# A chunked linear-attention and cosine-FFN kernel: first loads in thirds, no running minimum, the last output in halves, and another written order for the first stage

## The chip, the cores and the metric

The kernel runs on one core of one Trainium2 chip. The metric is the device time of one execution in microseconds (us), and lower is better. The core has five engines that run their own instruction streams and wait for each other through semaphores: TensorE (PE, matrix products), VectorE (DVE), ScalarE (ACT), GpSimd (POOL), and SyncE (SP), which here only issues DMA transfers. DMA transfers go through queues that feed 16 DMA engines. Matrix products write to PSUM, and everything else works from SBUF.

## The reference: what is computed

The first half is a recurrent attention over 768 steps for 4 batches and 8 heads with head size 48. Each step decays a 48x48 state and adds an outer product. The second half is a feed-forward layer with `h * cos(h)` between two matrix products, over 3072 tokens. All of it is fp32.

```python
for t in range(S):                                   # S = 768
    kt, vt, rt, wt = (k[:, :, t], v[:, :, t], r[:, :, t], w[:, :, t])
    cur = np.einsum('bhd,bhe->bhde', u[None] * kt, vt)
    y[:, :, t] = np.einsum('bhd,bhde->bhe', rt, state + cur)
    state = wt[:, :, :, None] * state + np.einsum('bhd,bhe->bhde', kt, vt)
...
x = y.transpose(0, 2, 1, 3).reshape(B * S, H * D)    # 3072 x 384
h = x @ w_in                                         # 384 -> 2048
return (h * np.cos(h)) @ w_out                       # 2048 -> 384
```

## The kernel before

**Tiling.** The 768 steps of a batch are cut into 6 chunks of 128 steps, so there are 24 chunks (numbered 0 to 23 in the order of work, with the batches of a pair alternating). Two chunks make a block of 256 tokens, and there are 12 blocks. Inside a chunk the recurrence becomes matrix products: cumulative products of the decays scale `r` and `k`, a 128x128 score matrix per head covers the chunk itself, and a 48x48 state per head carries what came before.

**Attention steps of a chunk,** by the short names that the order tables use:

- `load`: one DMA of 112 rows by 1541 floats (L185). A row holds `r` (512 floats), `k` (512) and the decays (517), in this order.
- `decay` (L203 to L220): `rkt` = r times k (L205, chunks 0 to 5 alone), a scan from the right for the decays to the chunk's end (`ee`, L208), the smallest product so far (`shrink`, L211), the whole product with a floor (`whole`, L213), its reciprocal (`inj`, L214), a second scan (L215), r times the second scan (L219), and k times the first (L220). L208 to L215 run on DVE. In the first stage L219 is on DVE and L220 on POOL.
- `diag`: products with `u` (PE, L226), a copy to `cd` (ACT), and two POOL instructions (L238) that lay them on a diagonal in `asb`.
- `a`: 8 products for the scores (PE, L258, written to `pa`), then two DVE instructions (L260) that put the masked scores into `asb`.
- `t`, `d`, `s`: the transpose of k (PE, L267, `pt`), the decayed state (`dd`), and the new state (PE, L285, `pst`).
- `o`, `p`, `x` of a block: own and past outputs (PE, L315 and L325, `py`), copied to `yf`, sent by DMA to the layout of the feed-forward layer (`xf`, L334 and L301), and split into a high and a low part (`xT`).

**Feed-forward units.** The 2048 hidden columns are 16 weight tiles of 128, and two tiles make a unit. `mm1` of a unit is 18 products (L382) into a PSUM tile `ph`. The gate of this unit follows: ACT rounds (L357), DVE subtracts (L358), ACT takes a sine and a square (L359, L360), and DVE multiplies (L361). Then ACT (or DVE later) takes the high part `gs`, and POOL the low part (L137, L140). `mm2` is 12 products (L398) into an accumulator. There are 96 units. They are numbered here from 0 in the order of mm1, and "gate 11" is L357 to L361 of unit 11.

**Weights.** A weight tile comes by DMA as doubles (`f` in the tables, tile `raw`, L147) and is converted once (`w`, L149 to L174). Two ACT instructions read the raw words (L159, L161), three DVE instructions build an fp32 (L163, L164, L171), ACT takes its high part and DVE its low part (L140). Raw tiles lie in slots that later hold converted weights. The raw tile of the last weight tile takes the slot of the raw tile before it, so its load waits until L164 and L161 have read that one.

**Stages and what sets the order.** In the first stage all 16 weight tiles are converted while blocks 0 and 1 take turns (`PAIR`), each unit running as soon as its weights are there. `START` is a table of step names, written by hand, that sets in which order the steps are recorded. PE and SP keep this order exactly. The instructions of DVE, ACT and POOL are placed by a scheduler from the same recording. After `START`, the table `PLAN` repeats for each block, and PE alone keeps its order.

While the two blocks take turns, `ph` has two PSUM banks, so mm1 of unit n writes where unit n-2 was, and waits for L361 of gate n-2. `mm1` runs ahead of `mm2` by a few units.

**The end.** After the last mm2 the two accumulators of the block are scaled and copied out (L405 to L412): chunk 0 of the block by ACT, the last chunk by DVE, each followed by one DMA from SP. A check near the end (`take_vote`, L486 to L496) tells by one number whether any decay product fell under a floor or any decay was above 1. If so, a slow path (`one_by_one`) recomputes everything. With these inputs it doesn't run.

## Time and profile before

| | |
|---|---|
| median of 3 runs | 572.2 us (572.1 to 574.48) |
| profiled execution, its own time | 578.14 us |
| span of the profiled execution | 576.3 us |
| mean granted TensorE clock | 0.961 |
| busy: PE, DVE, ACT, POOL | 525.4, 417.3, 248.5, 243.1 us |
| instructions | 11206 |
| DMA | 56.07 MB, mean 97 GB/s |

A profile shows one execution. "Busy" is the time in which an engine executed something. The granted clock is the share of its full speed that TensorE's clock was given, and matrix products take longer where it is low. A row of a timeline gives the start, the time from the first start to the last end, the engine, the line, the operation, what it writes and reads, and a count. In brackets stands the idle time just ahead of it with what ended it. A DVE instruction may start some 0.1 us before the one in front of it has ended, so the cost of a short one is read from the distance between starts.

### The profile page before, as it was taken

To read this page: it belongs to the slowest core of one execution; us is meant where nothing else is said; L and a number is where in the kernel's file an instruction comes from. 1 tells how busy PE (TensorE), PEld (TensorE's weight loads), DVE (VectorE), ACT (ScalarE), POOL (GpSimd) and SP (SyncE) were. 2 spreads that over 40 slices of the span, in tenths; PEclk is the share of its full clock that TensorE was granted. 3 is DMA by queue.
4 is the path that set the end of the run, shared out by engine and by line. 5 is a ranking of instruction groups with operands and counts; after the bars stand their busy time and mean duration, and the time that the engine had idled before them with its cause. 6 is when DMAs were issued, how large, how long until landed. Compare 5 with 4: busy or idle time off the path is not lost.

```text
span 576.3 us, 11206 instructions
## 1 busy us (share of the span) xinstructions
PE 525.4 (91%) x4420; PEld 501.7 (87%) x4420; DVE 417.3 (72%) x695; ACT 248.5 (43%) x419; POOL 243.1 (42%) x288
## 2 busy tenths in 40 slices
PE   3627888979999999899999999999899999999997
PEld 2516788979899999899899999899799999999996
DVE  6999999993786956955858847846857848836342
ACT  2355777852534342342442342342343342435441
POOL 2224238473534534532734633543444542313332
PEclk9966898986999999999999999999999999999999
DMA  8738384100434205215233025025015016310000
GB/s 262 237 107 318 96 305 116 54 3 28 145 118 134 74 28 155 52 39 158 59 110 105 2 75 160 1 61 172 3 53 155 1 43 229 115 42 16 27 1 31
DMA packets 22983, 56.07 MB, mean 97 GB/s; under 512 B 4240, under 2 KB 15120, under 8 KB 22928
## 3 DMA queue, kind: packets, MB, share of 16 engines
q1 hardware_dynamic: 20336, 53.55, 29.8%
q10 hardware_dynamic: 2592, 1.77, 1.2%
q8 instruction: 36, 0.59, 0.4%
q14 instruction: 19, 0.16, 0.1%
HBM read 45.87 MB, written 4.72 MB: 88 GB/s over the span
## 4 chain that ended last, share of the span: by engine, by line
PE 65%; DVE 16%; DMA 9%; issue 3%; SPq 2%; ACT 2%; POOL 1%; ACTq 0%; DVEq 0%; POOLq 0%
PE acc L398 26%; PE ph L382 26%; DMA xf<-yf 5%; PE py L315 5%; PE pa L258 4%; DMA tt<-tr 4%; DVE ee L208 2%; DVE tt L215 2%; PE py L325 2%; SPq L301 2%; DVE h L164 2%; DVE w L140 1%; DVE h L171 1%; DVE rr L361 1%; PE pt L267 1%
## 5 line engine op out<-in xcount | busy, mean ns | idle before, releaser
L140 POOL TENSOR_TENSOR gs<-rr,gs 128x256 fp32r<-128x256 f32 x192 | 165.3, 882 | 215.1 <-DVE gs L137 165.7
L382 PE MATMUL ph<-xT,w 128*128 128x256 f32 x1728 | 228.3, 288 | 18.0 <-ACT xT L137 10.0
L382 PEld LDWEIGHTS ph<-xT,w 128*128 128x128 f32 x1728 | 219.3, 194 | 21.9 <-ACT xT L137 10.1
L398 PE MATMUL acc<-w,gs 128*128 128x384 f32 x1152 | 222.9, 342 | 9.1 <-DVE gs L137 4.9
L398 PEld LDWEIGHTS acc<-w,gs 128*128 128x128 f32 x1152 | 200.3, 192 | 14.5 <-DVE gs L137 5.9
L359 ACT ACTIVATE rr<-rr 128x512 f32<-128x512 f32 x96 | 60.7, 632 | 120.5 <-DVE rr L358 120.5
L357 ACT ACTIVATE rr<-ph 128x512 int32<-128x512 f32 x96 | 56.5, 589 | 122.4 <-PE ph L382 82.1
L361 DVE SCALAR_TENSOR_TENSOR rr<-rr,ph 128x512 f32<-128x512 f32 x96 | 65.5, 682 | 49.7 <-ACT rr L360 49.0
L358 DVE SCALAR_TENSOR_TENSOR rr<-rr,ph 128x512 f32<-128x512 int32 x96 | 65.3, 680 | 33.9 <-ACT rr L357 33.7
L360 ACT ACTIVATE rr<-rr 128x512 f32<-128x512 f32 x96 | 60.6, 631 | 2.4
L238 POOL TENSOR_SCALAR_AFFINE_SELECT asb<-cd 128x512 f32<-128x512 f32 x48 | 35.0, 754 | 30.0 <-PE py L315 16.2
L137 DVE CAST gs<-rr 128x512 fp32r<-128x512 f32 x80 | 37.5, 469 | 9.9 <-PE acc L398 9.6
L208 DVE TENSOR_TENSOR_SCAN ee<-tt,one_e 112x516 f32<-112x516 f32 x24 | 30.4, 1267 | 15.6 <-DMA tt<-tr 15.2
L258 PE MATMUL pa<-tt 48*128 48x128 f32 x384 | 33.4, 311 | 3.5 <-DVE tt L219 3.5
L258 PEld LDWEIGHTS pa<-tt 48*128 48x128 f32 x384 | 28.2, 210 | 9.2 <-issue 3.0
L219 POOL TENSOR_TENSOR tt<-tt 112x512 f32<-112x512 f32 x18 | 24.1, 1337 | 27.8 <-DVE tt L215 27.8
L260 DVE COPY_PREDICATED asb<-mask,pa 128x512 f32<-128x512 uint8 x48 | 33.4, 731 | 0.9 <-PE pa L258 0.9
L215 DVE TENSOR_TENSOR_SCAN tt<-tt,inj 112x516 f32<-112x516 f32 x24 | 33.6, 1401 | 0.1
L315 PE MATMUL py<-asb,v 128*64 128x128 f32 (+1 forms) x384 | 27.3, 300 | 1.3 <-DVE asb L260 1.3
L315 PEld LDWEIGHTS py<-asb,v 128*64 128x64 f32 (+1 forms) x384 | 23.5, 143 | 3.9 <-DVE asb L260 2.6
L220 POOL TENSOR_TENSOR tt<-tt,ee 112x512 f32<-112x512 f32 x6 | 9.6, 1599 | 35.6 <-DVE ee L208 29.0
L231 DVE TENSOR_TENSOR rk<-rk 128x384 f32<-128x384 f32 x18 | 10.0, 559 | 15.9 <-DMA rk<-tn 15.9
(67 smaller groups left out, 353.5 us busy)
## 6 DMA issues: line engine op xcount, KB each, us to landing
tt<-tr SPq DMA_DIRECT2D x24, 674.2 KB, 6.1
raw<-wts SPq DMA_DIRECT2D x16, 768.0 KB, 8.2
rk<-tn SPq DMA_DIRECT2D x18, 384.0 KB, 3.9
v<-tn SPq DMA_DIRECT2D x24, 192.0 KB, 5.0
out<-ob SPq DMA_DIRECT2D x24, 192.0 KB, 2.0
ww<-w SPq DMA_DIRECT2D x6, 768.0 KB, 4.3
xf<-yf SPq DMA_DIRECT2D x30, 72.0 KB, 2.2
xf<-yf ACTq DMA_DIRECT2D x18, 72.0 KB, 4.2
```

The source lines that it names most:

```text
L140: E[name].tensor_tensor(out=out, in0=full, in1=high.bitcast(F32), op=ALU.subtract)
L208: nc.vector.tensor_tensor_scan(out=ee.rearrange("p a t -> p (a t)")[:, ::-1], data0=wp[:, 1:W129 + 1][:, ::-1], data1=one_e.rearrange("p a ...
L215: nc.vector.tensor_tensor_scan(out=wp[:, 0:W129], data0=wp[:, 0:W129], data1=inj.rearrange("p a t -> p (a t)"), initial=0.0, op0=ALU.mult, ...
L258: nc.tensor.matmul(out=pa[h][:, p], lhsT=a["k3"][rows(h), p], rhs=a["r3"][rows(h), p], start=True, stop=True)
L315: nc.tensor.matmul(out=py[SWAPPED[p]][ROW * o:ROW * o + m, n, p // 2], lhsT=a["v"][:, head_cols(p, h, m)], rhs=a["asb", h][:, p], start=n ...
L357: nc.scalar.activation(nn, ph, AF.Copy, scale=INV2PI / W_SCALE)
L358: nc.vector.scalar_tensor_tensor(out=rr, in0=nn, scalar=-2.0 * math.pi * W_SCALE, in1=ph, op0=ALU.mult, op1=ALU.add)
L359: nc.scalar.activation(rr, rr, AF.Sin, scale=0.5 / W_SCALE)
L360: nc.scalar.activation(rr, rr, AF.Square)
L361: nc.vector.scalar_tensor_tensor(out=rr, in0=rr, scalar=-0.5, in1=ph, op0=ALU.add, op1=ALU.mult)
L382: nc.tensor.matmul(out=ph[:, fi], lhsT=wgt[u * FU + fi][:, 0, a, kt * 128:(kt + 1) * 128], rhs=xT[:, b, kt], start=n == 0, stop=n == 3 * K ...
L398: nc.tensor.matmul(out=accs[i][j][:, :DM], lhsT=gs[:, a, fi, j * C:(j + 1) * C], rhs=wgt[u * FU + fi][:, 1, b], start=u == 0 and fi == 0 a ...
```

## The change

1. `shrink`, its start value and its instruction of each chunk (L211) are gone. Each chunk's whole product (L213) goes to its own columns of a tile `wholes` that stays, and the check at the end takes the smallest of them all in one instruction and compares it with the floor.
2. The loads of chunks 0 and 1 are three transfers each: the decays first, then `k`, then `r`. All other loads stay one transfer.
3. The last chunk's output is scaled in two halves at the same time, 192 columns by DVE and 192 by ACT, and each half has a DMA of its own, one issued by SP and one by ACT.
4. The table `START` has another order. Transposes `t2` and `t4`, scores `a4`, states `d0` and `d3`, some weight steps, one load and the outputs `o2` stand at other places.

```diff
+IN_PARTS = 2
...
-START = ["lv0 decay0 diag0 t0 load0 f load1 d0 f a0 f f diag1 w t1 decay2 o0 w a1 f diag2 d1 x0 f load3 p0 f",
+START = ["lv0 decay0 diag0 t0 load0 f load1 f d0 a0 f f diag1 w t1 decay2 o0 w a1 f diag2 d1 x0 f load3 p0 f",
...
-         "w lv4 w mm1 load6 mm1 lr6 t4 mm2 a4 w d4 mm2 w mm1 w mm1 w mm1 diag5 a5 w mm2 lv6 f mm2 mm1 d5 x4 o2",
+         "w lv4 w mm1 lr6 t4 mm2 a4 mm1 w d4 w load6 mm2 w mm1 w mm1 mm1 diag5 a5 mm2 lv6 w f mm2 mm1 d5 x4",
...
-    shrink = cst.tile([R, NP], F32, name="shrink")
-    nc.vector.memset(shrink, 1.0)
+    wholes = cst.tile([R, NG, NP], F32, name="wholes")
...
-        E["qt"].dma_start(out=tt, in_=tr[g])
+        for cols in ((1024, TRW), (512, 1024), (0, 512)) if j < IN_PARTS else ((0, TRW),):
+            E["qt"].dma_start(out=tt[:, slice(*cols)], in_=tr[g, :, slice(*cols)])
...
-        nc.vector.tensor_tensor(out=shrink, in0=shrink, in1=ee[:, :, 0], op=ALU.min)
-        whole = buf("whole", [R, NP], F32)
+        whole = wholes[:, a["j"]]
         nc.vector.tensor_single_scalar(out=whole, in_=ee[:, :, 0], scalar=LEAST, op=ALU.max)
...
-                        nc.vector.tensor_scalar(out=ob, in0=accs[i][j][:, :DM], scalar1=-2.0 / W_SCALE ** 2, scalar2=None, op0=ALU.mult)
+                        nc.vector.tensor_scalar(out=ob[:, :DM // 2], in0=accs[i][j][:, :DM // 2], scalar1=-2.0 / W_SCALE ** 2, scalar2=None, op0=ALU.mult)
+                        nc.scalar.activation(ob[:, DM // 2:], accs[i][j][:, DM // 2:DM], AF.Copy, scale=-2.0 / W_SCALE ** 2)
...
+                if at_end and j:
+                    nc.sync.dma_start(out=out[chunk * C:(chunk + 1) * C, :DM // 2], in_=ob[:, :DM // 2])
+                    nc.scalar.dma_start(out=out[chunk * C:(chunk + 1) * C, DM // 2:], in_=ob[:, DM // 2:])
+                else:
+                    E["qo"].dma_start(out=out[chunk * C:(chunk + 1) * C, :], in_=ob)
...
-        low = cst.tile([R, NP], F32, name="low")
-        nc.vector.tensor_single_scalar(out=low, in_=shrink, scalar=LEAST, op=ALU.is_lt)
+        least = cst.tile([R, 1], F32, name="least")
+        nc.vector.tensor_reduce(out=least, in_=wholes.rearrange("p g a -> p (g a)"), axis=mybir.AxisListType.X, op=ALU.min)
+        low = cst.tile([R, 1], F32, name="low")
+        nc.vector.tensor_single_scalar(out=low, in_=least, scalar=LEAST, op=ALU.is_le)
```

What moves is shown at three places. In the changed kernel the lines of the decay step carry other numbers: L206 is the old L205, and L209 the old L208.

**The first instructions of DVE,** after its constants are set. Before:

```order
L205 TENSOR_TENSOR rkt<-tt 112x512
L208 SCALAR_TENSOR_TENSOR ee<-tt,one_e 112x516
L211 TENSOR_TENSOR shrink<-shrink,ee 112x4
L213 TENSOR_SCALAR whole<-ee 112x4
L214 RECIPROCAL inj<-whole 112x4
L215 SCALAR_TENSOR_TENSOR tt<-tt,inj 112x516
L219 TENSOR_TENSOR tt<-tt 112x512
L109 TENSOR_REDUCE halves<-ident 96x2
L102 CAST mask<-maskf 128x512
L163 TENSOR_SCALAR h<-h 128x768
```

Now:

```order
L209 SCALAR_TENSOR_TENSOR ee<-tt,one_e 112x516
L213 TENSOR_SCALAR wholes<-ee 112x4
L214 RECIPROCAL inj<-wholes 112x4
L215 SCALAR_TENSOR_TENSOR tt<-tt,inj 112x516
L206 TENSOR_TENSOR rkt<-tt 112x512
L219 TENSOR_TENSOR tt<-tt 112x512
L110 TENSOR_REDUCE halves<-ident 96x2
L103 CAST mask<-maskf 128x512
L209 SCALAR_TENSOR_TENSOR ee<-tt,one_e 112x516
L163 TENSOR_SCALAR h<-h 128x768
```

Both scans of chunk 0 stand ahead of `rkt`, and chunk 1's first scan stands ahead of the first weight tile's L163 where it stood behind two of its instructions.

**PE between the scores of chunks 2 and 3.** `pc` and `pa` are chunk 3's diagonal products and the scores of chunk 2, then of chunk 3. `pt` is the transpose of chunk 2. Before:

```order
L226 MATMUL pc<-u_by_head,rkt 128x2 x4
L258 MATMUL pa<-tt 128x128 x8
L267 MATMUL pt<-ident,tt 128x112 x4
L258 MATMUL pa<-tt 128x128 x8
L315 MATMUL py<-asb,v 64x128
```

Now:

```order
L267 MATMUL pt<-ident,tt 128x112 x4
L382 MATMUL ph<-xT,w_176 128x256 x9
L382 MATMUL ph<-xT,w_236 128x256 x9
L226 MATMUL pc<-u_by_head,rkt 128x2 x4
L258 MATMUL pa<-tt 128x128 x16
L315 MATMUL py<-asb,v 64x128
```

The transpose went ahead of the first mm1, and the two sets of scores now follow each other.

**DVE between gate 10 and gate 11,** from behind L361 of gate 10 to L361 of gate 11. `w_1160` before and `w_1110` now are the low part of the last weight tile. Before:

```order
L260 COPY_PREDICATED asb<-mask,pa 128x512 x2
L163 TENSOR_SCALAR h<-h 128x768
L208 SCALAR_TENSOR_TENSOR ee<-tt,one_e 112x516
L164 SCALAR_TENSOR_TENSOR h<-raw,sign_bit,h 128x768
L211 TENSOR_TENSOR shrink<-shrink,ee 112x4
L213 TENSOR_SCALAR whole<-ee 112x4
L171 ISA h<-h,rd 128x1536
L214 RECIPROCAL inj<-whole 112x4
L358 SCALAR_TENSOR_TENSOR rr<-rr,ph 128x512
L215 SCALAR_TENSOR_TENSOR tt<-tt,inj 112x516
L140 TENSOR_TENSOR w_1160<-h,w_1160 128x2x384
L361 SCALAR_TENSOR_TENSOR rr<-rr,ph 128x512
```

Now:

```order
L171 ISA h<-h,rd 128x1536
L358 SCALAR_TENSOR_TENSOR rr<-rr,ph 128x512
L214 RECIPROCAL inj<-wholes 112x4
L209 SCALAR_TENSOR_TENSOR ee<-tt,one_e 112x516
L140 TENSOR_TENSOR w_1110<-h,w_1110 128x2x384
L215 SCALAR_TENSOR_TENSOR tt<-tt,inj 112x516
L361 SCALAR_TENSOR_TENSOR rr<-rr,ph 128x512
```

The two score copies (L260), L163, L164, a whole product and `shrink` no longer stand between the two gates. The copies, L163 and L164 now stand between gates 9 and 10. Chunk 7's whole product, reciprocal and second scan come behind gate 11; the reciprocal and the second scan that stand here now are chunk 6's.

Behind the first stage the written orders are the same in both kernels, but for a few instructions of one pair of chunks on DVE, the check near the end, and the last output.

7 lines of the change are left out of this document (3 added, 4 removed), and 6 rows, old and new, of the table START.

## The prediction

> **What bounds the kernel now.** I read the slices of the page first, then the clock by stretches, then the timelines around the one place where they all meet.
>
> ```profile
> PE   3627888979999999899999999999899999999997
> DVE  6999999993786956955858847846857848836342
> PEclk9966898986999999999999999999999999999999
> ```
>
> One slice is 14.4 us. DVE is full for nine slices, to about 130 us, and PE isn't. From the tenth slice on PE is full and DVE isn't. So the first 126 us belong to DVE and the rest to PE. Work taken from DVE pays in the first part alone, and there only where PE waits for it. The clock row has its last dip at the seam, in slice 10.
>
> ```profile
> 81.07:84.48 3.41, 2.08 (x18) 1.91 (x17) 3.41 (x9) 2.81 (x6) 0.00 (x0) 1.00 0.92 294
> 84.48:91.30 6.82, 6.82 (x52) 6.64 (x53) 6.82 (x10) 6.17 (x11) 5.68 (x4) 1.00 0.93 262
> 91.30:94.70 3.40, 1.57 (x12) 1.40 (x12) 3.40 (x5) 1.62 (x4) 3.40 (x4) 0.96 0.39 93
> 94.70:98.10 3.40, 3.40 (x18) 3.40 (x17) 3.32 (x4) 2.12 (x5) 3.40 (x3) 0.54 0.03 5
> ...
> 125.40:139.10 13.70, 12.83 (x58) 12.62 (x59) 8.62 (x16) 4.21 (x9) 4.82 (x5) 0.51 0.09 30
> ```
>
> The columns are the stretch, its length, busy time of PE, of PE's loads, DVE, ACT and POOL, then the granted clock. Where PE idled 1.33 us of 3.41, the clock stayed at 1.00. Where it idled 1.83 of 3.40, the next 3.4 us ran at about half. From 125.40 on it was at half for 13.7 us, behind the pause that is shown next. So here the point at which a pause costs clock lies between 1.33 and 1.83 us of such a stretch.
>
> ```profile
> 86.57 0.95 PE L226 MATMUL pc<-u_by_head,rkt 112*128 112x2 f32 x8
> ...
> 112.86 1.16 PE L258 MATMUL pa<-tt 48*128 48x128 f32 x16
> ...
> 120.45 2.25 PE L398 MATMUL acc<-w,gs 128*128 128x384 f32 x12
> 126.27 4.18 PE L382 MATMUL ph<-xT,w 128*128 128x256 f32 x18 [3.57 <-DVE rr L361]
> 130.25 1.70 PE L226 MATMUL pc<-u_by_head,rkt 112*128 112x2 f32 x8
> 131.88 2.40 PE L258 MATMUL pa<-tt 48*128 48x128 f32 x16
> 134.21 6.53 PE L398 MATMUL acc<-w,gs 128*128 128x384 f32 x24
> 140.58 2.31 PE L382 MATMUL ph<-xT,w 128*128 128x256 f32 x18
> ```
>
> This is the seam. mm1 of unit 13 waits 3.57 us for gate 11, then PE works without a gap but at half clock. The pause costs itself and then 4.18 - 2.31 on this mm1, 1.70 - 0.95 on `pc`, 2.40 - 1.16 on `pa` and 6.53 - 2 x 2.25 on two mm2, 5.9 us together. Nothing else is late here, so all of it is on the path. From here on PE sets the end, and whatever the start of this mm1 gains, the kernel gains.
>
> **The change part by part.** All is counted at the start of that mm1.
>
> *The removed minimum.*
>
> ```profile
> 7.79 0.17 DVE L211 TENSOR_TENSOR shrink<-shrink,ee 112x4 f32<-112x4 f32 x1
> 7.87 2.35 DVE L213 TENSOR_SCALAR whole<-ee 112x4 f32<-112x4 f32 x1
> ...
> 16.27 1.80 POOL L220 TENSOR_TENSOR tt<-tt,ee 112x512 f32<-112x512 f32 x1 [6.08 <-DVE ee L208]
> 16.95 1.14 DVE L211 TENSOR_TENSOR shrink<-shrink,ee 112x4 f32<-112x4 f32 x1
> ```
>
> ```profile
> L211 DVE TENSOR_TENSOR shrink<-shrink,ee 112x4 f32<-112x4 f32 x8 | 5.3, 667 | 0.0
> ```
>
> The last row is the group of these instructions in the first 135 us, 5.3 us over 8. This isn't what the removal saves. The instruction takes a step of 0.08 us when nothing is in its way (7.79 to 7.87). At 16.95 it took 1.14 us, until POOL's L220, begun at 16.27, was over at 18.07. At 7.87 the same delay fell on L213, 2.35 us. So the delay belongs to POOL's instruction, and the next one on DVE inherits it. I count 8 x 0.08 = 0.64 us, with 5.3 as the upper bound.
>
> *The order of DVE ahead of gate 11.* In the new order DVE does the same work ahead of L361 of gate 11, less the eight minima and less chunk 7's whole product, reciprocal and second scan.
>
> ```profile
> 116.88 0.66 DVE L361 SCALAR_TENSOR_TENSOR rr<-rr,ph 128x512 f32<-128x512 f32 x1
> 117.46 1.38 DVE L260 COPY_PREDICATED asb<-mask,pa 128x512 f32<-128x512 uint8 x2
> 118.73 0.54 DVE L163 TENSOR_SCALAR h<-h 128x768 int32<-128x768 int32 x1
> ...
> 120.33 0.99 DVE L164 SCALAR_TENSOR_TENSOR h<-raw,sign_bit,h 128x768 int32<-128x768 int32 x1
> ...
> 123.46 1.22 DVE L215 TENSOR_TENSOR_SCAN tt<-tt,inj 112x516 f32<-112x516 f32 x1
> 124.61 0.93 DVE L140 TENSOR_TENSOR w<-h,w 128x768 fp32r<-128x768 f32 x1
> 125.45 0.67 DVE L361 SCALAR_TENSOR_TENSOR rr<-rr,ph 128x512 f32<-128x512 f32 x1
> ```
>
> The scan's step is 124.61 - 123.46 = 1.15, the whole product's 0.08 and the reciprocal's about 0.1. With the minima that is **1.95 us** less. The order also evens the gates out. From gate 10 to gate 11 DVE took 125.45 - 116.88 = 8.57 us. Without the copies (118.73 - 117.46 = 1.27), L163 (about 0.5), L164 (about 0.9) and the short ones it is about 5.8. PE has an mm1 and an mm2 to do in this time, some 4.4 us warm. The pause ahead of the mm1 thus falls from 3.57 to about 1.4 us, next to the 1.33 that cost no clock.
>
> *A new wait on ACT and DVE.* Gate 10 now shares its stretch with the last weight tile, whose load can only start when L164 of the tile ahead has read the slot.
>
> ```profile
> 111.73 0.33 SPq L147 DMA_DIRECT2D raw<-wts  x1
> ```
>
> ```profile
> 117.46 0.93 ACT L159 ACTIVATE h<-raw 128x768 f32<-128x768 f32 x1 [1.88 <-DMA raw<-wts]
> ```
>
> From the issue to L159 it took 5.73 us, and L163 needs L159. In the new order only about 6.2 us of DVE work lie between that L164 and this L163: two low parts of weights (0.84 each), the two copies (1.27), a first scan (like the second, 1.15), L171 (like L164, 0.9), L361 and L358 (0.6 each). Against it stand 6.7 us for the load and L159. On ACT the sine of gate 10 also stands behind L159 and L161. DVE then waits 0 to 1.5 us. I take **0.7 lost**. Queued behind it are the L361 of gates 10 and 11, for which mm1 of units 12 and 13 wait.
>
> *The first loads.*
>
> ```profile
> tt<-tr SPq DMA_DIRECT2D x3, 674.2 KB, 11.3
> ```
>
> ```profile
> 2.68 0.43 SPq L185 DMA_DIRECT2D tt<-tr  x1
> ...
> 5.92 0.69 DVE L205 TENSOR_TENSOR rkt<-tt 112x512 f32<-112x512 f32 x1 [3.84 <-DMA tt<-tr]
> ...
> 10.96 0.89 ACT L159 ACTIVATE h<-raw 128x768 f32<-128x768 f32 x1 [2.23 <-DMA raw<-wts]
> ...
> 12.83 0.55 DVE L163 TENSOR_SCALAR h<-h 128x768 int32<-128x768 int32 x1
> ```
>
> The decays of chunk 0 land some 2 us ahead of the whole (a third of the bytes), and with that DVE starts near 4 instead of 5.92. But it doesn't keep this. Its next scan is chunk 1's. This load was issued at 2.68 and landed 11.3 later (the middle one of the three in the first 30 us), at 14.0, behind the first weight tile, which landed by 10.96. A third of these 3 us puts the decays of chunk 1 at 12.0. DVE then has the same list in front of it that it began at 12.83, so the gain is **0.8 us**. It is 0 if the third lands late, and no more than 1.9, the lead at the start.
>
> *The transpose between two scores.*
>
> ```profile
> 52.31 1.01 PE L267 MATMUL pt<-ident,tt 112*128 112x112 f32 x4 [2.91 <-DVE asb L260]
> ```
>
> ```profile
> 55.66 1.33 DVE L260 COPY_PREDICATED asb<-mask,pa 128x512 f32<-128x512 uint8 x2 [0.88 <-PE pa L258]
> ```
>
> DVE idled 0.88 us for the second scores, and a transpose of 1.01 us stood ahead of them. The second half of these scores still needs a bank that DVE's copy frees, so I take **0.7** of the 0.88.
>
> *The end.*
>
> ```profile
> 572.49 0.56 DVE L408 TENSOR_SCALAR ob<-acc 128x384 f32<-128x384 f32 x1 [3.68 <-PE acc L398]
> ```
>
> ```profile
> out<-ob SPq DMA_DIRECT2D x24, 192.0 KB, 2.0
> ...
> xf<-yf ACTq DMA_DIRECT2D x18, 72.0 KB, 4.2
> ```
>
> Half the columns save at most half of 0.56. A whole output took 2.0 us to land, and I leave it at that. From ACT's queue even 72 KB took 4.2, so up to 2.2 us may be lost. I take **0.2 gained**.
>
> *The clock.* If the pause stays under the point, the half clock goes. In this profile it cost 5.9 us. The stretches of 3.4 us don't move with the program: had one begun with the mm1, a single cold one (94.70 to 98.10) might have ended it, at 1.7. I take the middle, **3.8**.
>
> The sum is 1.95 - 0.7 + 0.8 + 0.7 + 0.2 + 3.8 = 6.75 us. The profiled execution, at 578.14, would be 571.4. It lies 5.9 us above the median of the three runs (572.2), and the share of the clock in that can't be seen, which is one more reason for the middle. Of the median the sum makes **565.4**.
>
> Which pauses count is where the Trainium skill ("TensorE: Matmul & The Clock Gate", What's actually happening) differs. It lets the clock fall after at least one idle window of about 3.4 us, in windows that run freely. The free windows agree with the rows; the length doesn't, since 1.83 us of idling was enough here. By its rule the new pause could not cost clock and the old one just could, and the sum would have 5.9 where it has 3.8: 563.3.
>
> **The rivals.**
>
> 1. *No pause counts any more, and the old one cost all of 5.9.* For it: the pause of 1.33 us. Against it: 1.4 is near 1.83, and a lost us on DVE closes the distance. Time: 572.2 - 2.95 - 5.9 = **563.3**. The clock page's rule would give this too.
> 2. *The pause shrinks but still costs clock.* Then the terms without the clock stay: 572.2 - 2.95 = **569.2**. For it: DVE's delays behind POOL are about 1.1 us each, and one of them between gates 10 and 11 makes 1.4 into 2.5.
> 3. *DVE's gain is used up.* Delays behind POOL and the wait for the last weight tile reach their bounds (another 0.8 and two delays of 1.1): 572.2 - 2.95 + 3.0, about **572**. That is also what is left if the removals do nothing beyond their 0.08 us steps and the order merely shuffles.
> 4. *Slower, by the last weight tile.* If its load takes 2 us longer than 5.7, gate 10 is late by 2, and the pause moves ahead of mm1 of unit 12, where it counts. It decides from 1.8 us on. This mm1 and the next mm2 then run cold: 4.2 instead of 2.3, and 4.4 instead of 2.25. mm1 of unit 13 starts about 2 us later than before, and the cold stretch after it is the same. With 1 us lost at the end by ACT's queue: **575.2**.
>
> **How the numbers follow.** The forecast (565.4) has 0.40, rival 1 0.13, rival 2 0.23, rival 3 0.13, rival 4 0.11. About 0.5% (2.9 us) is what a measurement of this kernel can tell from no change, so faster means under 569.3. The first two are faster, and of rival 2 a little over half: 0.40 + 0.13 + 0.13 = 0.66. Rival 4 is slower at 0.11. The rest, 0.23, is the same. The range runs from the 563.3 of rival 1 less 1.8 for a larger gain at the removed minima and first loads, 561.5, to 572.0, which takes in rival 2 and most of rival 3. The likeliest case by itself spans 563 to 568.
>
> **What would show it.** Right: the first scan starts near 4 us; the idle time ahead of unit 13's mm1 is below 2 us and the mm1 starts near 123.3; the clock there reads 1.00; PE's busy time falls by some 6 us while the counts stay. The removed minima's delays reappear on L213 or L164. Wrong: a low clock after 120 us, an L163 or an L361 of gate 10 with idle time ahead of it that a load or ACT ended, or a last DMA that lands over 2.5 us after its issue. If mm1 of unit 13 starts early and the time doesn't follow, then something behind it sets the end, and the reading of the first two rows was wrong.

## The result and the profile after

| | before | changed |
|---|---|---|
| median of 20 runs each | 573.7 us (570.05 to 577.79) | 568.8 us (562.83 to 572.63) |
| ratio | | 0.991, 95% interval 0.9888 to 0.9931 |
| profiled execution, its own time | 578.14 us | 567.22 us |
| span | 576.3 us | 565.4 us |
| mean granted TensorE clock | 0.961 | 0.970 |
| busy: PE, DVE | 525.4, 417.3 us | 522.6, 414.5 us |

The changed kernel is faster by 4.9 us, 0.9%. Here and below the ratios leave out executions that took over 1.5% longer than the fastest of the same kernel (up to four of a kernel; one, with the minimum back, took 656 us), while the medians have them all. The two profiled executions differ by 10.9 us, so more than half of what a comparison of the two traces shows isn't the change. The slices of the changed kernel's page:

```profile
PE   2637988989999999899999999999999999999997
DVE  5899899997787956856859758849858749836342
PEclk9965699999999999999999999999999999999999
```

The dip of the clock at the seam (slice 10) is gone. Another one, from 33 to 67 us, has become longer. DVE is still full to the ninth slice.

The seam on PE in the changed kernel's timeline:

```profile
118.64 2.38 PE L382 MATMUL ph<-xT,w 128*128 128x256 f32 x18
120.85 2.28 PE L398 MATMUL acc<-w,gs 128*128 128x384 f32 x12
124.82 2.37 PE L382 MATMUL ph<-xT,w 128*128 128x256 f32 x18 [1.69 <-DVE rr L361]
127.03 0.95 PE L226 MATMUL pc<-u_by_head,rkt 112*128 112x2 f32 x8
...
130.35 4.44 PE L398 MATMUL acc<-w,gs 128*128 128x384 f32 x24
134.62 2.29 PE L382 MATMUL ph<-xT,w 128*128 128x256 f32 x18
```

mm1 of unit 13 starts at 124.82 (126.27 before). Its pause is 1.69 us (3.57), and what stands behind it runs at its warm lengths: 2.37 instead of 4.18, 0.95 instead of 1.70, 4.44 instead of 6.53. Unit 14's mm1, 14.31 us behind unit 13's before, now is 9.80 behind it. The clock of the 14 us from 126 on, by stretch (length, busy PE, PE's loads, DVE, ACT, POOL, clock, DMA share, GB/s), before:

```profile
126.00:140.00 14.00, 13.73 (x63) 13.52 (x64) 8.02 (x15) 4.21 (x8) 5.01 (x7) 0.54 0.09 29
```

and changed:

```profile
126.00:140.00 14.00, 13.13 (x142) 12.31 (x141) 10.51 (x18) 6.09 (x12) 9.54 (x11) 1.00 0.09 29
```

PE was as busy, with 142 instructions instead of 63. The steady part behind the first stage differs too, though its instructions are nearly the same. The group of mm2 from there to the end (count, busy, mean ns, idle time ahead and what ended it), before:

```profile
L398 PE MATMUL acc<-w,gs 128*128 128x384 f32 x947 | 180.4, 338 | 5.3 <-DVE gs L137 4.9 <-POOL gs L140 0.3
```

and changed:

```profile
L398 PE MATMUL acc<-w,gs 128*128 128x384 f32 x960 | 184.1, 341 | 1.9 <-DVE gs L137 1.5 <-POOL gs L140 0.3
```

I put most of these 3.4 us of idling to the pair of executions, not to the change. A second look at the kernel before (the last experiment) took 574.7 us, 3.4 less than the first, with the same seam, and the same group idles 2.4 us there:

```profile
L398 PE MATMUL acc<-w,gs 128*128 128x384 f32 x960 | 182.6, 338 | 2.4 <-DVE gs L137 2.0 <-POOL gs L140 0.2
```

The other parts of the change, on DVE of the changed kernel:

```profile
3.85 1.23 DVE L209 TENSOR_TENSOR_SCAN ee<-tt,one_e 112x516 f32<-112x516 f32 x1 [1.78 <-DMA tt<-tr]
12.73 1.23 DVE L209 TENSOR_TENSOR_SCAN ee<-tt,one_e 112x516 f32<-112x516 f32 x1 [3.33 <-DMA tt<-tr]
24.95 1.33 DVE L260 COPY_PREDICATED asb<-mask,pa 128x512 f32<-128x512 uint8 x2 [1.38 <-PE pa L258]
30.09 1.15 DVE L213 TENSOR_SCALAR wholes<-ee 112x4 f32<-112x4 f32 x1
34.57 0.33 DVE L290 COPY sn<-pst 112x192 f32<-112x192 f32 x1
...
117.81 0.69 DVE L361 SCALAR_TENSOR_TENSOR rr<-rr,ph 128x512 f32<-128x512 f32 x1 [0.16 <-ACT rr L360]
...
124.02 0.65 DVE L361 SCALAR_TENSOR_TENSOR rr<-rr,ph 128x512 f32<-128x512 f32 x1
```

The first scan comes at 3.85 as forecast. Chunk 1's comes at 12.73, 0.7 later than I had worked out, and at 24.95 DVE waits 1.38 us for scores. The next instruction shown, the first new state, starts at 34.57, and so it does before:

```profile
34.57 0.33 DVE L290 COPY sn<-pst 112x192 f32<-112x192 f32 x1
```

So nothing of the early start is left at 34.57 us, which is also where the changed kernel with whole first loads has this row (see below). On PE the second set of scores no longer has a transpose ahead of it, and waits all the same, now for `r` times the second scan:

```profile
53.74 2.51 PE L258 MATMUL pa<-tt 48*128 48x128 f32 x16 [1.98 <-DVE tt L219]
```

At the end ACT's half stands behind DVE's half, not beside it:

```profile
561.60 0.36 DVE L408 TENSOR_SCALAR ob<-acc 128x192 f32<-128x192 f32 x1 [3.68 <-PE acc L398]
...
562.05 0.33 ACT L409 ACTIVATE ob<-acc 128x192 f32<-128x192 f32 x1 [1.00 <-DVE ob L408]
562.41 0.39 ACTq L415 DMA_DIRECT2D out<-ob  x1
```

From the first half's start to the second half's end it takes 0.78 us, where the whole copy took 0.56. From DVE's start to the end of the span it is 3.8 us in both kernels.

### The profile page after: what moved, and what is told of

The parts are those of the page before. It is cut to its first block, busy times and chain, and to the rows that moved or that the text cites. A ratio compares the mean times of both kernels' runs of the same rounds, so it can differ in the third digit from the quotient of the medians.

```text
span 565.4 us, 11194 instructions
## 1 busy us (share of the span) xinstructions
PE 522.6 (92%) x4420; PEld 496.8 (88%) x4420; DVE 414.5 (73%) x671; ACT 248.6 (44%) x420; POOL 241.4 (43%) x288
## 4 chain that ended last, share of the span: by engine, by line
PE 63%; DVE 17%; DMA 8%; issue 4%; SPq 3%; POOL 2%; ACT 1%; ACTq 0%; DVEq 0%; POOLq 0%
PE acc L398 26%; PE ph L382 25%; PE pa L258 4%; DMA xf<-yf 4%; PE py L315 4%; DMA tt<-tr 4%; DVE tt L215 2%; PE py L325 2%; SPq L301 2%; DVE ee L209 2%; DVE h L164 2%; DVE h L171 2%; POOL gs L140 1%; DVE w L140 1%; DVE rr L358 1%
## 5 line engine op out<-in xcount | busy, mean ns | idle before, releaser
L382 PE MATMUL ph<-xT,w 128*128 128x256 f32 x1728 | 225.6, 286 | 14.9 <-ACT xT L137 8.8
L382 PEld LDWEIGHTS ph<-xT,w 128*128 128x128 f32 x1728 | 216.3, 191 | 19.8 <-ACT xT L137 9.0
L398 PEld LDWEIGHTS acc<-w,gs 128*128 128x128 f32 x1152 | 197.2, 188 | 10.4 <-POOL gs L140 3.5
L361 DVE SCALAR_TENSOR_TENSOR rr<-rr,ph 128x512 f32<-128x512 f32 x96 | 65.6, 683 | 50.4 <-ACT rr L360 49.6
L209 DVE TENSOR_TENSOR_SCAN ee<-tt,one_e 112x516 f32<-112x516 f32 x24 | 31.0, 1291 | 18.7 <-DMA tt<-tr 17.9
L238 POOL TENSOR_SCALAR_AFFINE_SELECT asb<-cd 128x512 f32<-128x512 f32 x48 | 32.7, 705 | 28.0 <-PE py L315 15.5
L258 PE MATMUL pa<-tt 48*128 48x128 f32 x384 | 34.8, 312 | 5.8 <-ACT kn L137 2.8
L215 DVE TENSOR_TENSOR_SCAN tt<-tt,inj 112x516 f32<-112x516 f32 x24 | 34.9, 1455 | 0.1
L260 DVE COPY_PREDICATED asb<-mask,pa 128x512 f32<-128x512 uint8 x48 | 33.6, 731 | 1.4 <-PE pa L258 1.4
L231 DVE TENSOR_TENSOR rk<-rk 128x384 f32<-128x384 f32 x18 | 13.1, 726 | 14.9 <-DMA rk<-tn 14.9
```

The costliest lines, as they stand in the source:

```text
L209: nc.vector.tensor_tensor_scan(out=ee.rearrange("p a t -> p (a t)")[:, ::-1], data0=wp[:, 1:W129 + 1][:, ::-1], data1=one_e.rearrange("p a ...
L215: nc.vector.tensor_tensor_scan(out=wp[:, 0:W129], data0=wp[:, 0:W129], data1=inj.rearrange("p a t -> p (a t)"), initial=0.0, op0=ALU.mult, ...
L258: nc.tensor.matmul(out=pa[h][:, p], lhsT=a["k3"][rows(h), p], rhs=a["r3"][rows(h), p], start=True, stop=True)
L361: nc.vector.scalar_tensor_tensor(out=rr, in0=rr, scalar=-0.5, in1=ph, op0=ALU.add, op1=ALU.mult)
L382: nc.tensor.matmul(out=ph[:, fi], lhsT=wgt[u * FU + fi][:, 0, a, kt * 128:(kt + 1) * 128], rhs=xT[:, b, kt], start=n == 0, stop=n == 3 * K ...
L398: nc.tensor.matmul(out=accs[i][j][:, :DM], lhsT=gs[:, a, fi, j * C:(j + 1) * C], rhs=wgt[u * FU + fi][:, 1, b], start=u == 0 and fi == 0 a ...
```

## The experiments

Ratios are to the kernel before on the same chip, with 95% intervals. Names: T is the prediction's theory, that the order brings the pause at the seam under the point where it costs clock, and that the rest is worth little.

### The order alone

The kernel before with the new `START` and nothing else.

```
...
-         "s1 f a3 mm1 w f w load5 f t3 decay4 mm2 decay1 lv5 mm1 mm1 w diag4 mm2 f mm1 decay5 mm1 mm2 mm1 mm2",
+         "s1 f a3 mm1 w f w load5 f t3 decay4 mm2 decay1 lv5 mm1 mm1 w diag4 f mm2 mm1 decay5 mm1 mm2 mm1 mm2",
...
```

> The kernel before with the new order of the first stage and nothing else: the running minimum, the whole first loads and the whole last output stay. T (all of the gain is the order's: less VectorE work ahead of gate 11 brings the pause ahead of unit 13's mm1 under the point at which the clock falls): the pause is 1.7 to 2.1 us, the clock is 1.00 from there on, and the ratio to before is 0.990 to 0.994, that of the whole change (0.991). Rival A (the removed minima and the split loads carry part of it): the pause stays over 2.5 us, the clock falls to half at about 125 us, and the ratio is 0.997 to 1.000. Rival B (the gain is no seam's, but the phase that the steady part falls into): the pause and the clock there come out as under T, and the ratio is not bound to them.

Measured: 571.19 us, ratio 0.9961 (0.9932 to 0.9991). That is between T and rival A, and the interval reaches into both: a gain of 0.1 to 0.7%, where the whole change has 0.9%. On PE:

```profile
119.56 4.18 PE L382 MATMUL ph<-xT,w 128*128 128x256 f32 x18 [3.21 <-DVE rr L361]
123.54 3.13 PE L398 MATMUL acc<-w,gs 128*128 128x384 f32 x12
126.51 2.31 PE L382 MATMUL ph<-xT,w 128*128 128x256 f32 x18
```

The pause is still there, one unit earlier. Unit 12's mm1 waits 3.21 us for gate 10, and the clock is at half from 118.6 to 125.4. The new table by itself moves the pause and halves the cold stretch behind it, 6.8 us where it was 13.7. In this profile PE starts unit 16's mm1 at 154.90 us, before at 160.25, which is more than the median gained. The written order is that of the changed kernel, but DVE's isn't written. The scheduler places it, and with the minimum and the whole loads in it, it sorts DVE otherwise: from gate 9 to gate 10 it took 118.76 - 110.47 = 8.29 us, in the changed kernel 117.81 - 111.06 = 6.75.

### The rest without the order

```
...
-         "s1 f a3 mm1 w f w load5 f t3 decay4 mm2 decay1 lv5 mm1 mm1 w diag4 f mm2 mm1 decay5 mm1 mm2 mm1 mm2",
+         "s1 f a3 mm1 w f w load5 f t3 decay4 mm2 decay1 lv5 mm1 mm1 w diag4 mm2 f mm1 decay5 mm1 mm2 mm1 mm2",
...
```

This is the changed kernel with the old table. It keeps the removed minimum, the split loads and the halved output.

> The whole change with the old order of the first stage: no running minimum, split first loads and halved last output stay. T (these three are worth nothing without the order): the pause ahead of unit 13's mm1 stays between 2.9 and 3.6 us, the half clock returns at about 125 us, and the ratio is 0.998 to 1.001. Rival A (the removed minima and the loads pay): 0.994 to 0.997, and if the pause falls under 2 us, 0.991.

Measured: 576.66 us, ratio 1.0061 (1.0025 to 1.0096), slower than the kernel before. All the expectations missed it. The pause ahead of unit 13's mm1 had grown to 5.61 us, and gate 11 came 3.5 us later (128.94). The size fits a standstill over 40 us earlier:

```profile
76.81 6.05 POOL L140 TENSOR_TENSOR gs<-rr,gs 128x256 fp32r<-128x256 f32 x2 [4.67 <-ACT gs L137]
...
87.60 0.69 DVE L358 SCALAR_TENSOR_TENSOR rr<-rr,ph 128x512 f32<-128x512 int32 x1 [3.80 <-ACT rr L357]
```

A pair of POOL's low parts took 6.05 us, and later DVE, which is what sets the end of this stage, stood still for 3.80 us. This stall comes back below. It doesn't account for the lost 3 us in this profile: of the 6.8 us at half clock PE worked only 3.8, and it started unit 16's mm1 at 159.81 us, no later than before (160.25). Where they are lost stays open.

### Filling the pause of the kernel before

16 products of a constant bf16 tile, 128 x 512, go to two free banks between the mm2 and unit 13's mm1. DVE's work is as before.

```
-         "w lv4 w mm1 load6 mm1 lr6 t4 mm2 a4 w d4 mm2 w mm1 w mm1 w mm1 diag5 a5 w mm2 lv6 f mm2 mm1 d5 x4 o2",
+         "w lv4 w mm1 load6 mm1 lr6 t4 mm2 a4 w d4 mm2 w mm1 w mm1 w mm2 z16 mm1 diag5 a5 w mm2 lv6 f mm2 mm1 d5 x4 o2",
...
+        for part in range(2):
+            pz = bank("a", [C, 512], "pz")
+            for _ in range(n // 2):
+                nc.tensor.matmul(out=pz, lhsT=dull[:, :128], rhs=dull, start=True, stop=True)
```

> The kernel before, all parts, order and minimum unchanged, with 16 matmuls on a constant tile (128 x 512, bf16, results not used) put on TensorE between the mm2 and unit 13's mm1, where TensorE pauses 3.57 us. They compute nothing of the output. T (it is TensorE's pause that lowers the clock, and the low clock, not the pause, is most of the cost): unit 13's mm1 still starts at 126 to 127 us, but the granted clock stays 1.00 after it, the stretch to unit 16's mm1 falls from 34.0 to about 29 us, and the ratio is 0.990 to 0.993. Rival A (the late gate itself costs, whatever the clock): the clock may stay at 1.00, but the ratio is 0.998 to 1.003, since nothing of VectorE's work is gone. Rival B (the clock falls for other reasons than the pause): half clock after 125 us as before, ratio 1.000 or over.

Measured: 569.79 us, ratio 0.9931 (0.9901 to 0.996). In the timeline and in the clock of the stretch behind it:

```profile
121.75 3.63 PE L514 MATMUL pz<-dull 128*128 128x512 bf16 x16
126.30 2.38 PE L382 MATMUL ph<-xT,w 128*128 128x256 f32 x18 [0.93 <-DVE rr L361]
```

```profile
126.00:140.00 14.00, 13.70 (x144) 13.25 (x148) 8.91 (x17) 6.75 (x12) 8.59 (x11) 1.00 0.10 29
```

Gate 11 is as late as before (L361 at 125.48 and 125.45), and mm1 starts at 126.30 instead of 126.27. Yet from there to unit 16's mm1 it takes 28.5 us instead of 34.0, and the median falls by 3.9. So the low clock behind the pause is worth 3.9 us by itself (2.3 to 5.7 by the interval), and nothing that DVE does has to change for it. T is right on this point, and both rivals fall.

### A longer pause in the changed kernel

```
+        if split and n_gates[0] == 12:
+            for _ in range(3):
+                nc.vector.scalar_tensor_tensor(out=rr, in0=rr, scalar=0.0, in1=rr, op0=ALU.mult, op1=ALU.add)
```

> The changed kernel with three more VectorE operations in gate 11 (each adds zero times a tile to it, so that nothing changes but VectorE's time, some 1.8 us) ahead of unit 13's mm1. T (there is a point of the pause between 1.7 and 3.6 us from which the clock falls): the pause grows from 1.69 to about 3.5 us, the half clock returns for some 14 us behind it, and the time is 568.8 + 1.8 + 4 to 6 = 574 to 577 us, a ratio to the kernel before of 1.000 to 1.006. Rival (no such point; only the waiting counts): +1.8 us and full clock, a ratio of 0.994 to 0.996.

Measured: 574.79 us, ratio 1.003 (0.9991 to 1.0069), where T put it. The half clock returned, though for half the time that T said, and the pause came out larger than meant:

```profile
130.05 3.80 PE L389 MATMUL ph<-xT,w 128*128 128x256 f32 x18 [5.95 <-DVE rr L368]
```

The clock was at half from 126.4 to 133.2, and PE worked 3.2 us of that; the rest lies in the pause. The scheduler spread the three operations over 122.58 to 126.96, and the sine of gate 11 waits for the last. This profile also has the stall of the run above (6.06 us for a pair of POOL's, then 3.79 us on DVE). So not all of the 6 us over the changed kernel is the added work and the clock, and the run doesn't separate them. The better comparison is with a run further down that has the same stall and not the three instructions (570.1): 4.7 us for some 1.8 us of work, of which 2.7 are there when PE starts unit 16's mm1 (159.83 and 157.09). PE's work at half clock is about the same in both, 3.2 and 3.4 us, so the difference isn't one of the clock.

### Whole first loads in the changed kernel

```
-IN_PARTS = 2
+IN_PARTS = 0
```

I now had a second theory, S: an edit is worth what it does to the order in which DVE's work is sorted ahead of gates 10 and 11.

> The changed kernel with the first loads whole again. S (each edit is worth what it does to the order in which VectorE's work is sorted ahead of gates 10 and 11): VectorE's program has 10 operations of some 7.4 us in gate 10's stretch and 9 of some 5.4 in gate 11's, near the changed kernel's 7.3 and 6.0, so no pause over 2.5 us comes up and the time is that of the changed kernel within 0.3%, 567.5 to 570.5 us. Rival (split loads pay by the earlier first decays, as the prediction had it): 0.8 to 1.9 us later at the seam and 569.6 to 571 us, with VectorE's early groups later by as much as late as 35 us into the span.

Measured: 568.41 us, ratio 0.9917 (0.989 to 0.9944), the changed kernel's, as S had it. The split loads bring nothing that could be measured. On PE:

```profile
118.51 2.36 PE L382 MATMUL ph<-xT,w 128*128 128x256 f32 x18 [0.75 <-DVE rr L361]
120.71 2.28 PE L398 MATMUL acc<-w,gs 128*128 128x384 f32 x12
124.64 2.37 PE L382 MATMUL ph<-xT,w 128*128 128x256 f32 x18 [1.66 <-DVE rr L361]
```

The pause is split over two units, and neither part costs clock. The 12 executions lie between 567.1 and 571.3, the changed kernel's 20 between 562.8 and 572.6.

### The minimum back in the changed kernel

```
+        nc.vector.tensor_tensor(out=shrink, in0=shrink, in1=ee[:, :, 0], op=ALU.min)
```

> The changed kernel with the running minimum back (split loads, halved output and new order stay). Rival (the prediction's sizes: eight operations of 0.08 us each): +0.6 us, 569.4 us. S: with the minimum VectorE's program has the two scans of 1.2 and 1.75 us ahead of gate 10's L361 again, as in the run with the new order alone, so the pause moves to unit 12's mm1 and is 2.5 to 3.5 us, the clock falls to half there, and the time is that of the order-only run: 570.5 to 572 us, ratio to the kernel before 0.994 to 0.997.

Measured: 575.3 us, ratio 1.0034 (1.0005 to 1.0064). Eight instructions of 0.08 us each make some 6 us, more than either theory had. S was right about the place, a pause ahead of unit 12's mm1 with half clock behind it:

```profile
122.91 3.36 PE L384 MATMUL ph<-xT,w 128*128 128x256 f32 x18 [2.58 <-DVE rr L363]
```

Some 45 us earlier DVE stands still, and the timeline has the chain that leads there, from POOL to PE, ACT and DVE:

```profile
71.17 4.89 POOL L141 TENSOR_TENSOR gs<-rr,gs 128x256 fp32r<-128x256 f32 x2 [5.70 <-ACT gs L138]
...
76.11 1.01 PE L400 MATMUL acc<-w,gs 128*128 128x384 f32 x2 [2.96 <-POOL gs L141]
76.92 0.95 PE L269 MATMUL pt<-ident,tt 112*128 112x112 f32 x4
77.91 0.48 ACT L138 COPY kn<-pt 128x384 f32<-128x384 f32 x1 [3.78 <-PE pt L269]
78.28 0.63 ACT L362 ACTIVATE rr<-rr 128x512 f32<-128x512 f32 x1
...
78.94 0.69 DVE L363 SCALAR_TENSOR_TENSOR rr<-rr,ph 128x512 f32<-128x512 f32 x1 [3.47 <-ACT rr L362]
```

POOL's two low parts of gate 1 took 4.89 us. The last two products of the mm2 wait for them, and a transpose is queued behind these. ACT's copy of the transpose waits, and gate 2's square is queued behind that copy. DVE waits 3.47 us for the square. The same two instructions of POOL took 2.31 us in the kernel before:

```profile
70.66 2.31 POOL L140 TENSOR_TENSOR gs<-rr,gs 128x256 fp32r<-128x256 f32 x2 [6.91 <-ACT gs L137]
```

So besides the sorting at the seam there is a second price, the standstill that follows where POOL's low parts take long. It isn't the minimum's alone: the changed kernel has one of the same kind in a second profile (see the run with two tiles). PE starts unit 16's mm1 at 157.86 us here, at 153.67 in the profile of the result and at 157.09 in that second one. So of the 6 us the profiles find 4.2 or 0.8 in the first stage, by which one is compared, and the rest isn't explained.

### The minimum gone, alone

The kernel before without the running minimum, with `wholes` in its place.

```
-        nc.vector.tensor_tensor(out=shrink, in0=shrink, in1=ee[:, :, 0], op=ALU.min)
-        whole = buf("whole", [R, NP], F32)
+        whole = wholes[:, a["j"]]
```

> The kernel before with the running minimum gone and nothing else changed. Rival (the prediction's sizes): -0.6 us, ratio 0.999. S: VectorE's program now has two scans of the second kind (L215) and the first u product (L231) ahead of gate 11's L361, some 10.5 us of work where it was 9.5, so the pause ahead of unit 13's mm1 grows to 4 to 6 us and the kernel is slower: ratio 1.002 to 1.008, near the old-order run's 1.006.

Measured: 571.44 us, ratio 0.9969 (0.9935 to 1.0002), so S, which had it slower, was wrong, and the rival's 0.6 us lies inside the interval, as no change at all just does. The pause stayed at 3.54 us ahead of unit 13's mm1, which started at 126.55, and the clock was at half for 13.7 us behind it. Gate 11's last instruction came at 125.75, 0.3 us later than before, where S had the pause grow. What the 1.7 us are, if they are real, these profiles don't show.

### A fill in the wrong place

12 constant products ahead of unit 13's mm1 in the changed kernel, and two tiles for the last output's halves.

```
-         "w lv4 w mm1 lr6 t4 mm2 a4 mm1 w d4 w load6 mm2 w mm1 w mm1 mm1 diag5 a5 mm2 lv6 w f mm2 mm1 d5 x4",
+         "w lv4 w mm1 lr6 t4 mm2 a4 mm1 w d4 w load6 mm2 w mm1 w mm1 z12 mm1 diag5 a5 mm2 lv6 w f mm2 mm1 d5 x4",
```

> The changed kernel with 12 matmuls on a constant tile (not used for the output) in the pause of 1.69 us ahead of unit 13's mm1, and the last output's halves in two tiles, so that ScalarE's half needs not wait for VectorE's. Theory: the pause is at the edge of what costs clock, so that some executions of the changed kernel still pay there; filled, the slow executions go: 566.5 to 568 us; the last halves start within 0.1 us of each other and the tail is 0.3 us shorter. Rival (the changed kernel's pause costs no clock in any execution, and the fill delays mm1): 568.5 to 569.5 us.

Measured: 570.5 us, ratio 0.9954 (0.992 to 0.9988). A miss of mine: the mm2 ahead of this mm1 is recorded together with it, so the fill stood in front of the mm2 and delayed it by 2.4 us. The time is above both expectations. This profile has the stall too, and the run to compare it with is the one with the two tiles alone, further down, which also has it: 570.1 us, no measurable difference. Unit 13's mm1 starts at 127.45 here and at 127.17 there, and no half clock follows it here.

### The split loads alone

The kernel before with the first loads in three transfers. The third theory, N, follows from the stalls above.

```
-        E["qt"].dma_start(out=tt, in_=tr[g])
+        for cols in ((1024, TRW), (512, 1024), (0, 512)) if j < IN_PARTS else ((0, TRW),):
+            E["qt"].dma_start(out=tt[:, slice(*cols)], in_=tr[g, :, slice(*cols)])
```

> The kernel before with the first loads in three transfers and nothing else changed. Rival (the prediction's step: the first scan earlier, 0 to 1.9 us gained): ratio 0.997 to 1.000. New theory N (an edit is worth what the re-sorted order makes GpSimd's subtracts and the gates wait): VectorE's order up to gate 4 is the same as in the run with the minimum back, where GpSimd's two subtracts of gate 1 took 4.89 us instead of 2.3 behind VectorE's unbroken row of work and VectorE then stood still for 3.47 us ahead of gate 2's last operation. The same shows here, a pair of subtracts of over 4 us and a VectorE pause of 3 to 4 us near 75 to 79 us, and the time is 3 to 5 us over the kernel before: ratio 1.005 to 1.009.

Measured: 576.13 us, ratio 1.0044 (1.0008 to 1.0079), slower. The place and the sizes of the stall are those that N gave, and the ratio lies just under the 1.005 that it gave:

```profile
72.09 4.89 POOL L141 TENSOR_TENSOR gs<-rr,gs 128x256 fp32r<-128x256 f32 x2 [7.55 <-ACT gs L138]
...
79.86 0.69 DVE L363 SCALAR_TENSOR_TENSOR rr<-rr,ph 128x512 f32<-128x512 f32 x1 [3.47 <-ACT rr L362]
```

Gate 11's last instruction is 4.6 us later than before (130.05), and the pause ahead of unit 13's mm1 is 4.37 us. But the half clock lasts 3.4 us where it was 13.7, and PE starts unit 16's mm1 at 160.84 us, only 0.6 later than before. So N named the stall, and this profile doesn't show that the stall is the 2.7 us. An edit that only lets data arrive earlier made the kernel slower. With it the scheduler chose another order for DVE, from the first instructions on; that this order is the reason is argued, not shown.

### Two tiles for the last output

```
+                    ob2 = buf("rr", [C, DM], F32, "ob2")
-                        nc.scalar.activation(ob[:, DM // 2:], ...)
+                        nc.scalar.activation(ob2[:, DM // 2:], ...)
```

> The changed kernel with the halves of the last output in two tiles. If ScalarE's half waits for VectorE's only because both write one tile: ScalarE's half starts within 0.1 us of VectorE's, the last transfer starts 0.3 to 0.4 us earlier, and the time is that of the changed kernel less 0.3 us, 568.3 to 568.7 us. Rival (the wait has another cause): ScalarE's half still starts some 0.4 us later, and nothing is gained.

Measured: 570.11 us, ratio 0.9947 (0.9909 to 0.9985). The rival was right: ACT's half (564.12) still starts 0.45 us behind DVE's (563.67), so one shared tile isn't the reason. Both halves also read one accumulator, in PSUM; that wasn't tried.

Up to the last output this is the changed kernel, and so it is a second look at its first stage:

```profile
77.73 6.05 POOL L140 TENSOR_TENSOR gs<-rr,gs 128x256 fp32r<-128x256 f32 x2 [4.66 <-ACT gs L137]
...
88.53 0.69 DVE L358 SCALAR_TENSOR_TENSOR rr<-rr,ph 128x512 f32<-128x512 int32 x1 [3.80 <-ACT rr L357]
...
127.17 3.79 PE L382 MATMUL ph<-xT,w 128*128 128x256 f32 x18 [1.80 <-DVE rr L361]
```

```profile
127.70:131.10 3.40, 3.40 (x19) 3.40 (x17) 3.40 (x7) 1.73 (x4) 0.93 (x2) 0.50 0.00 0
```

Here the changed kernel's own order has the stall, and its pause of 1.80 us is followed by 3.4 us at half clock. Gate 11's last instruction starts at 126.37, later than in the kernel before (125.45). In the profile of the result the same pair of POOL's went like this:

```profile
79.23 3.10 POOL L140 TENSOR_TENSOR gs<-rr,gs 128x256 fp32r<-128x256 f32 x2 [3.80 <-ACT gs L137]
```

3.10 us, no standstill, and 1.69 us of pause without a price. Of the four profiles that have this order up to gate 11 three show the stall (this one, the longer pause, the misplaced fill); the one of the result is the exception. PE starts unit 16's mm1 at 157.09 us here and at 153.67 there, and in the two profiles of the kernel before at 159.93 and 160.25. At this point the change gains 6.6 us by the first looks and 2.8 by the second ones, and the 4.9 that were measured lie between.

### Whole loads, a fill behind the mm2, two tiles

```
-         "w lv4 w mm1 lr6 t4 mm2 a4 mm1 w d4 w load6 mm2 w mm1 w mm1 mm1 diag5 a5 mm2 lv6 w f mm2 mm1 d5 x4",
+         "w lv4 w mm1 lr6 t4 mm2 a4 mm1 w d4 w load6 mm2 w mm1 w mm1 mm2 z6 mm1 diag5 a5 mm2 lv6 w f mm2 mm1 d5 x4",
```

This goes with `IN_PARTS = 0` and `ob2` in the changed kernel.

> The changed kernel with whole first loads, two tiles for the last output, and 6 matmuls on a constant tile (1.4 us, not used for the output), this time behind the mm2 that they were ahead of, in the pause of 1.7 us ahead of unit 13's mm1. Theory (that pause still lowers the clock in some executions): 567 to 568 us, and no execution over 571. Rival (it does not): 568 to 569 us, that of the run with whole loads less 0.3 at most.

Measured: 568.15 us, ratio 0.9926 (0.9896 to 0.9955), 566.3 to 570.7.

```profile
123.15 1.24 PE L523 MATMUL pz<-dull 128*128 128x512 bf16 x5
124.84 2.37 PE L382 MATMUL ph<-xT,w 128*128 128x256 f32 x18 [0.45 <-DVE rr L361]
```

(The trace has five of the six products.) It is 0.3 us from the run with whole loads, which these intervals can't tell from none, and so the run doesn't decide between theory and rival. No kernel here is measurably better than the changed one.

### A second look at the kernel before

> The kernel before, unchanged, for a second look at its clock. If the pause of 3.57 us lowers the clock in every execution, the half clock follows unit 13's mm1 for 13.7 us here too. If it depends on the execution (its mean clock runs from 0.957 to 0.997 over the timed executions, and 0.997 leaves room for one stretch of 3.4 us), the half clock there is shorter or absent, while the pause is the same.

Measured: 574.7 us in one execution.

```profile
126.26 4.18 PE L382 MATMUL ph<-xT,w 128*128 128x256 f32 x18 [4.38 <-DVE rr L361]
```

```profile
124.40:138.10 13.70, 11.84 (x54) 11.63 (x55) 9.34 (x17) 4.60 (x9) 5.46 (x5) 0.50 0.10 30
```

The seam is nearly the same: mm1 at 126.26 (126.27) and half clock for 13.7 us, while the pause is 4.38 us, since PE was done earlier. Gate 11's L361 stands at 125.44, in the first profile at 125.45, and with the filled pause at 125.48. With this order DVE's row of work sets the time to a few hundredths. With the changed kernel's it doesn't: there gate 11 stands at 124.02 in one profile and at 126.37 in another.

This profile also has a stretch that idles as long as the one of the prediction with 1.83 us, in the same place of the same kernel:

```profile
90.30:93.71 3.41, 1.57 (x14) 1.40 (x13) 3.41 (x6) 1.60 (x4) 3.41 (x3) 1.00 0.73 155
93.71:97.12 3.41, 3.41 (x25) 3.41 (x26) 3.41 (x5) 3.38 (x6) 3.41 (x4) 1.00 0.05 14
```

It idles 1.84 us, and the clock behind it stays at 1.00. So the point at which idling costs clock isn't a sharp one.

## Why the prediction was right, and where not

The forecast was 565.4 us from a median of 572.2, a ratio of 0.988 with a range of 0.981 to 1.000; measured was 0.991, 568.8 us. The forecast is 3.4 us too low, and the measured time lies nearer to rival 2 (569.2). Two numbers read from the profiles sort the runs roughly: when DVE ends gate 11, and how long the clock is at half at the seam. The start of unit 16's mm1 stands beside them; it is where PE itself is, well behind the seam.

| kernel | L361 of gate 11 starts | half clock at the seam | unit 16's mm1 starts | median | median less the first column |
|---|---|---|---|---|---|
| filled pause | 125.48 | 0 | 154.75 | 569.8 | 444.3 |
| changed, whole loads | 123.82 | 0 | 152.89 | 568.4 | 444.6 |
| the same, filled, two tiles | 124.02 | 0 | 153.10 | 568.2 | 444.1 |
| fill in the wrong place | 126.10 | 0 | 155.88 | 570.5 | 444.4 |
| changed | 124.02 | 0 | 153.67 | 568.8 | 444.8 |
| changed, two tiles | 126.37 | 3.4 | 157.09 | 570.1 | 443.7 |
| minimum back | 128.54 | 3.4 | 157.86 | 575.3 | 446.8 |
| split loads alone | 130.05 | 3.4 | 160.84 | 576.1 | 446.1 |
| longer pause | 129.25 | 6.8 | 159.83 | 574.8 | 445.5 |
| order alone | 124.77 | 6.8 | 154.90 | 571.2 | 446.4 |
| rest without the order | 128.94 | 6.8 | 159.81 | 576.7 | 447.8 |
| minimum gone alone | 125.75 | 13.7 | 160.59 | 571.4 | 445.7 |
| before | 125.45 | 13.7 | 160.25 | 573.7 | 448.2 |

Without a cold stretch the last column is 444.1 to 444.8. With one it is up to some 4 us more, in one row a little less. In the rows of the longer pause and of the rest without the order, about half of the 6.8 us lies in the pause itself. The starts and the clock are of one execution and the median of many, so single rows are no better than two or three microseconds. The row of the minimum gone alone shows it: PE is as late as before, and the median is 1.7 us below that of the kernel before on the same chip.

Order, minimum and split loads were run in all eight combinations (four of them with the halved output, which gained nothing at the end). With whole loads the parts add up within the intervals: the order alone has 0.9961, the removed minimum alone 0.9969, and both together 0.9917, where the product is 0.9930. Splitting the loads made three of the four kernels slower: the kernel before by 0.4%, the one with the new order by 0.7% (0.9961 to 1.0034), the one without the minimum by 0.9% (0.9969 to 1.0061). The fourth it left where it was (0.9917 to 0.991). So the gain is that of the order and the removed minimum together, and the split loads are no part of it. T, which gave nearly all of it to the order, has about half by these medians.

Point by point:

- *What bounds it.* Right. DVE sets the first 126 us, PE the rest, and a gain at unit 13's mm1 is a gain of the kernel: the filled pause won 3.9 us by the clock alone. The reverse, that a later start loses as much, isn't shown as cleanly.
- *The clock, 3.8 us.* Right in size: 3.9 by the filled pause. In the changed kernel the cold stretch is gone in one profile and 3.4 us long in another. Also the point: 1.69 us of pause was free, 1.80 was followed by 3.4 us at half clock, both inside the 1.33 to 1.83 that the rows of before gave. It isn't sharp, since 1.84 us of idling in one stretch was free too. (The stretch that gave 1.33 was read 0.3 us late. Where the clock's own change at 94.40 puts it, from 80.75 to 84.16, it idles 1.14.) The rule that I had set against it, the Trainium skill's "TensorE: Matmul & The Clock Gate" (What's actually happening), at least one idle window of about 3.4 us, is contradicted by the 1.80. The length of the cold stretch doesn't follow the pause: 13.7 us behind 3.57 and 4.38, 6.8 behind 5.61, 3.4 behind 4.37. What ends it is open.
- *DVE ahead of gate 11, 1.95 us.* Too much. From gate 10 to gate 11 it is 124.02 - 117.81 = 6.21 us instead of about 5.8, and mm1 of unit 13 started 1.45 us earlier, not the 2.75 that the terms ahead of it add up to. The missing part is the next two points. All this is of the profile of the result. In the run with two tiles, whose order is the same up to there, gate 11 came 0.9 us later than before (126.37) and the mm1 started at 127.17, so that in this execution the term was no gain at all.
- *The first loads, 0.8 gained.* Failed. The first scan came at 3.85 as forecast, but chunk 1's decays landed 0.7 late, then DVE waited for scores, and at 34.57 us both kernels stood at the same instruction at the same time. I had let DVE go on with "the same list" from there. The list isn't the same: with the loads split it is sorted anew, and the split loads alone made the kernel slower by 2.7 us.
- *The transpose, 0.7 gained.* Failed. The scores behind it wait for `r` times the scan from DVE (1.98 us), which I hadn't looked at.
- *The wait for the last weight tile, 0.7 lost.* It cost 0.16 us ahead of gate 10's L361. Rival 4, which rested on it, fell.
- *The last output, 0.2 gained.* Nothing: the halves run one behind the other.
- *The removed minimum, 0.64 us.* The reasoning on its delays held (the 1.15 us are on L213 at 30.09 now). The price isn't settled: in the kernel before it lies between no change and 3.7 us, which has room for 0.64, and in the changed kernel the minimum makes some 6. My bound of 5.3 had been made from the instructions' own time. With the minimum back DVE's order is another one from 42 us on; that the order makes the price is my reading.

The net by the profile of the result is -1.45 at the start of unit 13's mm1 and some -3.9 from the clock, 5.3 against 4.9 measured. The sum of the prediction was larger for the most part by the 0.8, 0.7 and 0.2 that didn't come. That this net fits so well is partly luck: the other three profiles of this order have the stall, and the one of them that is the same program up to the last output starts the mm1 later than before. Rival 2, 569.2 with a pause that shrinks but still costs clock, is what some executions of the changed kernel do, as the second look at its seam shows. How many do, no run shows.

What is left open: why POOL's pair took 4.89 to 6.05 us. In all profiles that have it DVE worked without a gap from the pair's start nearly to its end. But so it did in the profile of the result, where the pair took 3.10 us. In the profiles with whole loads no pair there is over 4 us and no standstill follows. That the two contend is my reading; no run took DVE's work away from that place. The Trainium skill ("SBUF — State Buffer", SBUF: two separate sides) has a lock that VectorE and GpSimd share, held for a whole instruction of GpSimd's, or of VectorE's if that reads two inputs from SBUF or runs in one of its two-port modes. The runs here don't test it; the pair of 6.05 us outlasted eight of VectorE's instructions, and a lock held for one of them at a time doesn't explain that by itself.

## What to carry to other kernels

Where a scheduler places an engine's work, an edit can be worth much more or less than the instructions that it removes or the data that it brings earlier, since another order comes out; compare that order, and try each part alone and left out, before adding parts up. A pause of TensorE can cost as much by the clock behind it as by itself, and filling it with products that nobody uses gives that part back without touching what is late. When one execution of each kernel is compared, a second profile of the same kernel tells how much of the difference is the change.
